# Top-32 attention and two feed-forward layers on one core: rounding moved to GpSimd, early scores finished sooner, first block's last steps put first

## The chip, the cores and the metric

The kernel runs on one core of a Trainium2 chip. The metric is the device time of one execution in microseconds, lower is better. Engines are called as in the profile: PE (TensorE matmul), PEld (its weight loads), DVE (VectorE), ACT (ScalarE), POOL (GpSimd) and SP (SyncE, which issues the DMAs).

## The reference

```python
def _attn_ref(q, k, v):                       # (4, 8, 576, 64) each
    scores = scale * np.matmul(q, k.transpose(0, 1, 3, 2))
    kth = np.partition(scores, -top_k, axis=-1)[..., -top_k:-top_k + 1]      # top_k = 32
    scores = np.where(scores >= kth, scores, -1000000000.0)
    attn = np.exp(scores - np.max(scores, axis=-1, keepdims=True))
    attn = attn / (np.sum(attn, axis=-1, keepdims=True) + 1e-09)
    return np.matmul(attn, v)
x = attn_out as (2304, 512)
x = np.maximum(x @ w_in, 0.0) ** 2 @ w_out            # layer 0: (512, 2048), (2048, 512)
h = x @ w_in2; return np.maximum(0.01 * h, h) @ w_out2    # layer 1
```

The weights come as 64-bit floats; the kernel rebuilds 32-bit ones on the chip.

## The kernel before

**Precision.** Every float32 operand of the large matmuls is used as two rounded parts, a high one (`split_hi`: the value written in the rounded format) and a low one (value minus high part, on POOL). `split_hi` runs on ACT where its flag is set, else on POOL. The flag is set for the head pairs with index in `HI_SET`, here the indices 0 to 15.

**Attention.** Four batches, four head pairs each. Rows are cut into units (`UNITS`); a unit and a head pair make a `uh`, a `uh` has tiles of 128 score rows by 576 columns, two tiles are a pair. There are 72 pairs, and each has 16 slots. In 14 of them DVE searches the 32 largest of a row, 8 at a time: per tile four `DVE.max` (L829) and three `DVE.match_replace` (L831). The loop over slots is the program's backbone; everything else is put on a slot with `at(slot, fn)`. What follows a pair's search: `shifts` (POOL, L288 and L289, the tile nb), `drop` (ACT, L295) and `expo_sum` (ACT, L299), `recip` (sum on POOL, L303; 1/sum on DVE, L304), `pt_main` and `pt_left` (PE transposes, ACT copies to PT), `av` (PE, values), `x_out` (DVE product xn, L428; ACT xh, L429; POOL xl, L432).

**Scores.** Batches 0 and 1 are direct: their scores are made 30 slots (`DLEAD`) before their search. Batches 2 and 3 (`EARLY`) are made ahead, spread over the slots of `FILL`, evicted to the tile stage and stored to DRAM (sd), to be loaded later. The rounded keys are KT (direct) and KTa (early). In PSUM the early scores have `SPB` banks (sp), the direct ones of batch 0 have `SDB` (sd), and three banks (att) serve the rest.

**Layers.** The 2304 rows are taken in blocks of 512, 256, 384, 512, 256, 384. Once a block's x is complete (`ready`), `moe(j, layer)` adds 16 steps for each layer: 12 matmuls into h (L575), activation on ACT, the low part gl on POOL, and 3 matmuls for each of `na` accumulators (L618 or L620). Block 0 consists of units 0 and 1, thus of the pairs 0 to 15; its slot `rslot[0]` is that of the last `x_out`. In the first 32 steps the weights are new: each has two raw tiles (wraw, 512 KB) that go through two ACT passes (L509, L510), two DVE passes (L514, L515), an ACT rounding (L519) and a POOL subtraction (L521), and are stored to DRAM (wd) for later blocks. The weights of the steps 0 and 1 are converted before the block is ready (`convert_now`).

**Order.** On each engine the instructions run in the order of the program. That order is made when the kernel is built, by a scheduler that takes priorities: what an event emits has an offset of `SOON` (100).

Of the kernel before, what the change touches and what calls it, by code (L numbers as in the profile page):

```python
# [8 lines left out]
F = mybir.dt.float32  # L9
R = mybir.dt.float32r  # L10
U = mybir.dt.uint32
AF = mybir.ActivationFunctionType
OP = mybir.AluOpType
# [6 lines left out]
H_SCALE = 2.0 ** -112  # L20


L_SCALE = 2.0 ** -29 * (1 - 2.0 ** -21)
L_BIAS = -0.499999
# [7 lines left out]
BLOCKS = [512, 256, 384, 512, 256, 384]  # L32
# [8 lines left out]
NATIVE = 3  # L41

EARLY = (2, 3)
FILL = (2, 245)
KPB = 2
NST = 3
SDB = 2
SPB = 3

NS = 6  # L50
NE = 4
# [1 line left out]
WCB = 4  # L53
# [3 lines left out]
DLEAD = 30  # L57
LEAD = 24

SOON = 100  # L60
CONVP = 30

HI_SET = (0, 1, 2, 3, 4, 5, 6, 7, 8, 9, 10, 11, 12, 13, 14, 15)
KLO_D = ((0, 0), (0, 1))
QLO_D = (0,)

# [5 lines left out]
def topk_attention_moe_moe2_kernel(  # L72
# [10 lines left out]
    B, NHP, _, _, S = q.shape  # L83
    D = v.shape[-1]
    P = 128
    DM, NF = 2 * NHP * D, w1.shape[0]
    NK = DM // P
    HALF = S // 2
# [5 lines left out]
    PE, ACT, DVE, POOL, SP = nc.tensor, nc.scalar, nc.vector, nc.gpsimd, nc.sync  # L94

    const = ctx.enter_context(tc.tile_pool(name="const", bufs=1))
    pool = ctx.enter_context(tc.tile_pool(name="work", bufs=2))
# [9 lines left out]
    def behind(key):  # L107

        return tc.issue_after(cur[key].ins) if key in cur else ExitStack()

    def split_hi(dst, src, act=False):
        if act:
            ACT.activation(dst, src, AF.Copy)
            return
        POOL.tensor_scalar(dst, src, 1.0, 1.0, op0=OP.mult, op1=OP.mult)
# [7 lines left out]
    uhs = []  # L123
    tiles = []
    for u in units:
        for hp in range(NHP):
            n = u["n"]
            uh = dict(u=u, hp=hp, n=n, b=u["b"], first=(u["t0"] == 0), ti=len(tiles), idx=len(uhs),
                      c0=P * (hp % 2) if n == 64 else 0)
            offs = (W - 64 - n, 64)  # L130
            for t in range(2 * n // P):
                lo, hi = t * P, t * P + P
# [11 lines left out]
    def direct(uh):  # L144
        return uh["b"] not in EARLY
# [4 lines left out]
    def split(uh):  # L150
        return uh["u"]["i"] >= NATIVE
# [4 lines left out]
    stage_psum = ahead_ctx.enter_context(tc.tile_pool(name="stage_psum", bufs=1, space=bass.MemoryType.PSUM))  # L156
    qsets = []
    for i in range(4):
        x = const if i < 2 else ahead
# [28 lines left out]
    def at(slot, fn, *a):  # L188
        events.setdefault(slot, []).append((fn, a))


    KT = {}

# [64 lines left out]
    def scores(t, half):  # L258
        uh = t["uh"]
        d = uh["qs"]  # L260
        kt = KT[uh["b"], uh["hp"]]
        if half == 0:
            if direct(uh):
                t["s"] = sbufs[t["i"] % NS]
            else:
                t["s"] = ahead.tile([P, S], F, tag="stage", name="stage", bufs=NST)
        ks = slice(half * HALF, (half + 1) * HALF)
        mm = [(x[:, h, c:c + P], kt[:, h, ks]) for h, c in t["parts"] for x in d]
        if not direct(uh):
            ps = stage_psum.tile([P, 512], F, tag="sp", name="sp", bufs=SPB)  # L270
        elif uh["b"] == 0:
            ps = stage_psum.tile([P, 512], F, tag="sd", name="sd", bufs=SDB)
        else:
            ps = bank()
        for i, (l, r) in enumerate(mm):
            PE.matmul(ps[:, 0:HALF], lhsT=l, rhs=r, start=i == 0, stop=i == len(mm) - 1)  # L276
        ACT.activation(t["s"][:, ks], ps[:, 0:HALF], AF.Copy)  # L277
        if half == 1 and not direct(uh):
            t["sd"] = dram.tile([P, S], F, tag=f"sd{t['i']}", name=f"sd{t['i']}")
            SP.dma_start(t["sd"], t["s"])  # L280
# [188 lines left out]
    wraw = {}  # L469

    def w_alloc(i):
        wi = pool.tile([P, 2, 512], R, tag="wi", name="wi", bufs=3)
        wo = pool.tile([P, 2, 512], R, tag="wo", name="wo", bufs=4)
        wt[i] = (wi, wo)
        return wi, wo
# [16 lines left out]
    def w_convert(i):  # L492
        g = w_convert_steps(i)
        while True:
            with tc.high_priority(offset=CONVP):
                if next(g, 1):
# [3 lines left out]
    def w_convert_steps(i):  # L500
# [3 lines left out]
        for raw, w in zip(wraw.pop(i), w2):  # L504
# [16 lines left out]
            POOL.tensor_tensor(w[:, 1, :], c, w.bitcast(F)[:, 0, :], op=OP.subtract)  # L521
            yield 0

    def w_store(i):
        if i >= len(steps) or not fresh[i]:
            return
        wi, wo = wt[i]
        d = wdram[steps[i][1:]]
        SP.dma_start(d[:, 0:2, :], wi.bitcast(F))
        SP.dma_start(d[:, 2:4, :], wo.bitcast(F))  # L530
# [123 lines left out]
    for uh in uhs:  # L654
        b, hp, i = uh["b"], uh["hp"], uh.get("di")
        z = score_slot(uh["ti"])
# [49 lines left out]
    for n, key in enumerate(keys):  # L706
        ks = [(0, load_k, (*key, held[key]))]
# [9 lines left out]
        if n + 1 < len(keys):  # L717
            nk = keys[n + 1]
            ks = [(0, load_k, (*nk, held[nk]))]
# [7 lines left out]
    for _ in range(2):  # L727
        at(FILL[0] - 1, request)
    done = 0
    for w, fn, args in fill:  # L730
        at(FILL[0] + (FILL[1] - FILL[0]) * done // total, fn, *args)
        done += w

    pairs = []
    for p in range(NPAIRS):
        pr = dict(t=tiles[2 * p:2 * p + 2], p=p)
        pairs.append(pr)
        z = 16 * p
        for i, t in enumerate(pr["t"]):
            if direct(t["uh"]):  # L740
                at(z - DLEAD + 5 * i, scores, t, 0)
                at(z - DLEAD + 2 + 5 * i, scores, t, 1)
            else:
                at(z - LEAD + i, load_s, t)
            if i == 0:
                at(z + 14, shifts, pr)
            at(z + 14 + i, drop, pr, i)
            at(z + 16 + i, expo_sum, pr, i)
            if split(t["uh"]):
                at(z + 20 + i, norm, pr, i)  # L750
            at(max(z + 20 + 3 * i, z + 21 + i), pt_main, t)
        at(z + 18, recip, pr)
        at(z + 26, pt_left, pr)
    rslot = [None] * len(blocks)
# [8 lines left out]
    for uh in uhs:  # L763
        if split(uh):
            za, z = 16 * (uh["lastA"] // 2) + 30, 16 * (uh["last"] // 2) + 30
            at(za, av_split, uh, 0)
            at(z + 2, av_split, uh, 1)
            z += 4
            at(z, x_out, uh, (0, 1))
            rmark(uh, z)  # L770
            continue
        apart = uh["n"] > P and uh["n"] % P and uh["ti"] % 2 == 0
        for hs in ((0,), (1,)) if apart else ((0, 1),):
            z = 16 * (uh["lastA"] // 2 if hs == (0,) else uh["last"] // 2) + 30
            nq = 2 * len(hs)
            for i in range(nq):
                at(z + i, av, uh, hs, i)
            at(z + nq, x_out, uh, hs)
        z += nq
        if uh["u"]["i"] == NATIVE - 1 and uh["hp"] == NHP - 1:  # L780
            at(z, open_late)
        rmark(uh, z)
# [6 lines left out]
        for _ in w_convert(i):  # L789
            pass  # L790

    at(rslot[0] - 80, w_raw, 0)
    at(rslot[0] - 80, w_raw, 1)
    at(rslot[0] - 28, convert_now, 0)
    at(rslot[0] - 27, w_raw, 2)
    at(rslot[0] - 14, convert_now, 1)
    at(rslot[0] - 13, w_raw, 3)
    at(rslot[0] - 10, w_store, 0)

    active = []  # L800
    credit = 0.0
# [11 lines left out]
    last = max(events)  # L813
    while slot <= last:
        p, i = divmod(slot, 16)
        if slot >= 0 and p < NPAIRS:
            pr = pairs[p]
# [6 lines left out]
            x = i % 2  # L824
            t = pr["t"][x]
# [9 lines left out]
        for fn, a in events.pop(slot, []):  # L835
            nr = len(ready)
            with tc.high_priority(offset=SOON):
                fn(*a)
# [66 lines left out]
```

## Time and profile before

| | before |
|---|---|
| median of 3 runs | 1211.68 us (1209.5 to 1212.38) |
| profiled execution, its own time | 1210.15 us |
| its span, first to last instruction | 1208.4 us |
| PE busy | 94% |
| DVE, ACT, POOL busy | 78%, 67%, 57% |
| mean granted TensorE clock | 0.98 |

Busy shares are averages over stages that differ: the attention of the first block alone, then attention and layers together, then layers alone. A matmul's recorded duration is longer than the time that it takes of PE, since matmuls overlap; the distance between starts tells that time. The profiled execution is 1.5 us below the median of the runs.

### The profile page before, as it was taken

How to read it: one execution, taken by the hardware profiler on the slowest of the kernel's cores; microseconds unless marked ns; L12 is line 12 of the kernel's file. 1: busy time of each engine (PE TensorE's matmuls, PEld its weight loads, DVE VectorE, ACT ScalarE, POOL GpSimd, SP SyncE). 2: the span in 40 equal slices, each digit the busy share in tenths (PEclk: the TensorE clock that was granted, in tenths of full speed). 3: DMA queues.
4: the chain of work that ended last, by engine and by line, in shares of the span. 5: the costliest groups of instructions: out<-in, count | busy, mean ns of one | idle time of the engine just before them, and what ended most of it. 6: DMA issues, size and time to landing. Idle time of an engine off the chain costs nothing.

```text
span 1208.4 us, 20261 instructions
## 1 busy us (share of the span) xinstructions
PE 1135.8 (94%) x6388; PEld 992.5 (82%) x6388; DVE 946.5 (78%) x1944; ACT 807.5 (67%) x1831; POOL 682.8 (57%) x982
## 2 busy tenths in 40 slices
PE   4988987999889999999999999999999999999998
PEld 3776765887678779988999898888788899999997
DVE  7999899868988999999999999999999930110122
ACT  6988898878998986766656666555666653334322
POOL 7765564877878876556666665555565644004300
PEclk9899897999999999999999999999999999999999
DMA  9765566779989888879988888776676679779974
GB/s 307 255 217 192 192 220 222 267 233 333 342 280 319 305 267 263 296 269 384 355 293 290 298 272 286 221 227 226 201 239 211 199 255 369 253 253 341 356 256 135
DMA packets 110522, 323.25 MB, mean 268 GB/s; under 512 B 17488, under 2 KB 25680, under 8 KB 110416
## 3 DMA queue, kind: packets, MB, share of 16 engines
q1 hardware_dynamic: 107776, 317.24, 77.5%
q10 hardware_dynamic: 2640, 4.72, 1.1%
q8 instruction: 52, 0.85, 0.3%
q14 instruction: 54, 0.44, 0.1%
HBM read 254.54 MB, written 67.37 MB: 266 GB/s over the span
## 4 chain that ended last, share of the span: by engine, by line
PE 71%; ACT 11%; DVE 7%; DMA 6%; issue 2%; POOL 1%; ACTq 0%; SPq 0%; POOLq 0%; DVEq 0%
PE h L575 29%; PE acc L620 14%; PE acc L618 14%; PE att L408 4%; PE att L313 4%; DVE m L829 3%; PE att L397 3%; DVE w L831 3%; DMA wraw<-in_w_dram 2%; DMA sd<-stage 2%; ACT stage L277 1%; ACT e L299 1%; ACT e L295 1%; ACT s L277 1%; PE sp L276 1%
## 5 line engine op out<-in xcount | busy, mean ns | idle before, releaser
L575 PE MATMUL h<-xh,wi 128*128 128x512 f32 (+2 forms) x1280 | 349.9, 345 | 13.4 <-ACT gb L597 4.2
L829 DVE MAX8 m<-w 128x8 f32<-128x576 f32 x432 | 311.9, 748 | 1.1
L575 PEld LDWEIGHTS h<-xh,wi 128*128 128x128 f32 x1280 | 227.5, 191 | 42.6 <-ACT gb L597 5.8
L831 DVE MATCH_REPLACE8 w<-m,w 128x576 f32<-128x576 f32 x288 | 213.5, 744 | 0.8
L575 PE MATMUL h<-xl,wi 128*128 128x512 f32 (+2 forms) x640 | 207.6, 342 | 0.6 <-DVE xl L632 0.6
L601 POOL TENSOR_TENSOR gl<-ga,gh 128x512 fp32r<-128x512 f32 (+2 forms) x160 | 162.7, 1017 | 37.9 <-ACT gh L600 32.1
L618 PE MATMUL acc<-gh,wo 128*128 128x512 f32 (+2 forms) x768 | 156.8, 340 | 0.0
L620 PE MATMUL acc<-wo,gh 128*128 128x512 f32 x576 | 152.5, 399 | 2.9 <-ACT gh L600 2.7
L598 POOL TENSOR_TENSOR ga<-ga,gb 128x512 f32<-128x512 f32 (+2 forms) x80 | 81.4, 1017 | 130.6 <-ACT gb L597 127.3
L618 PEld LDWEIGHTS acc<-gh,wo 128*128 128x128 f32 x768 | 126.5, 189 | 11.0 <-ACT gh L586 0.2
L575 PEld LDWEIGHTS h<-xl,wi 128*128 128x128 f32 x640 | 121.4, 191 | 12.3 <-DVE xl L632 1.1
L295 ACT ACTIVATE e<-s,m 128x576 f32<-128x576 f32 x144 | 111.7, 779 | 18.6 <-DVE m L829 13.4
L620 PEld LDWEIGHTS acc<-wo,gh 128*128 128x128 f32 x576 | 104.3, 189 | 24.1 <-ACT gh L600 5.0
L829 DVE MAX8 m<-s 128x8 f32<-128x576 f32 x144 | 104.1, 748 | 12.5 <-ACT s L277 6.1
L299 ACT ACTIVATE e<-e,nb 128x576 f32<-128x576 f32 x144 | 111.0, 774 | 3.2 <-POOL nb L289 2.8
L587 POOL TENSOR_TENSOR ga<-ga 128x512 f32<-128x512 f32 (+2 forms) x80 | 66.1, 827 | 78.1 <-ACT gh L586 72.8
L831 DVE MATCH_REPLACE8 w<-m,s 128x576 f32<-128x576 f32 x144 | 107.1, 744 | 0.6
L313 PE MATMUL att<-ident,e 128*128 128x128 f32 x576 | 90.8, 281 | 13.7 <-ACT e L299 5.1
L313 PEld LDWEIGHTS att<-ident,e 128*128 128x128 f32 x576 | 70.0, 143 | 27.4 <-ACT e L299 10.1
L308 POOL TENSOR_SCALAR e<-e,rc 128x576 f32<-128x576 f32 x108 | 79.8, 749 | 22.5 <-DVE rc L304 21.1
L585 ACT ACTIVATE ga<-h 128x512 f32<-128x512 f32 (+2 forms) x80 | 39.0, 488 | 77.4 <-PE h L575 71.9
L618 PE MATMUL acc<-gl,wo 128*128 128x512 f32 (+2 forms) x384 | 87.7, 345 | 0.1
(94 smaller groups left out, 2136.7 us busy)
## 6 DMA issues: line engine op xcount, KB each, us to landing
wi<-wd SPq DMA_DIRECT2D x160, 512.0 KB, 5.0
wo<-wd SPq DMA_DIRECT2D x160, 512.0 KB, 5.2
wraw<-in_w_dram SPq DMA_DIRECT2D x64, 512.0 KB, 6.0
sd<-stage SPq DMA_DIRECT2D x72, 288.0 KB, 2.9
s<-sd SPq DMA_DIRECT2D x72, 288.0 KB, 4.6
wd<-wi SPq DMA_DIRECT2D x32, 512.0 KB, 5.4
wd<-wo SPq DMA_DIRECT2D x32, 512.0 KB, 5.9
kraw<-in_k_dram SPq DMA_DIRECT2D x16, 576.0 KB, 5.4
```

The costliest lines, as they stand in the source:

```text
L295: ACT.activation(t["e"], t["s"], AF.Prelu, bias=pr["m8"][:, i, 31:32], scale=-1.0, alpha=0.125 / FAR)
L299: ACT.activation(e, e, AF.Exp, bias=pr["nb"][:, i:i + 1], scale=-FAR, accum_out=pr["sum"][:, i:i + 1])
L308: POOL.tensor_scalar(e, e, pr["rc"][:, i:i + 1], 1.0, op0=OP.mult, op1=OP.mult)
L313: PE.transpose(ps[:, j * P:(j + 1) * P], t["e"][:, j * P:(j + 1) * P], ident)
L575: PE.matmul(h[:, 0:n], lhsT=wi[:, w, c * P:(c + 1) * P], rhs=x[c][y][:, 0:n], start=cnt == 0, stop=cnt == 3 * NK - 1)
L587: POOL.tensor_tensor(a[:, 0:n], a[:, 0:n], a[:, 0:n], op=OP.mult)
L598: POOL.tensor_tensor(a[:, 0:n], a[:, 0:n], b[:, 0:n], op=OP.subtract)
L601: (DVE if j >= GLD else POOL).tensor_tensor(gl[:, 0:n], a[:, 0:n], gh.bitcast(F)[:, 0:n], op=OP.subtract)
L618: PE.matmul(acc[c][:, 0:n], lhsT=wo[:, w, cs], rhs=g[:, 0:n], start=first, stop=last)
L620: PE.matmul(acc[c], lhsT=g[:, cs], rhs=wo[:, w, :], start=first, stop=last)
L829: cur["dve"] = DVE.max(out=m8[:, x, 8 * r:8 * r + 8], in_=t["s"] if r == 0 else t["w"])
L831: cur["dve"] = DVE.match_replace(out=t["w"], in_to_replace=m8[:, x, 8 * r:8 * r + 8], in_values=t["s"] if r == 0 else t["w"], imm_value=NEG)
```

## The change

- `HI_SET` shrinks to the indices 0 and 1. The high parts of queries, direct keys and values with higher indices are made on POOL.
- The early scores are done by slot 215 instead of 245. A tile's two halves lie in one PSUM tile of two banks, and one ACT instruction evicts both. `SPB` is 2 such tiles (4 banks, before 3), `SDB` is 1 bank (before 2).
- Pair 15 (`first_done`) has its `shifts`, `drop`, `expo_sum`, `recip`, `pt_main` and `pt_left` emitted at its slots 13 and 14, with priority 800. Its `uh` is taken in two halves (`apart`), the second with priority. `rslot[0]` becomes slot 257 (before 274).
- The conversion of the weights of steps 0 and 1 is cut in two: the ACT passes at the slots 218 and 232, with the result in an sp tile, and the rest (`lead_bits`: DVE passes, rounding on POOL, subtraction) at slot 253.

```diff
-FILL = (2, 245)
+FILL = (2, 215)
-SDB = 2
-SPB = 3
+SDB = 1
+SPB = 2
+URGENT = 800
-HI_SET = (0, 1, 2, 3, 4, 5, 6, 7, 8, 9, 10, 11, 12, 13, 14, 15)
+HI_SET = (0, 1)
+    def urgent(fn):
+        def run(*a):
+            with tc.high_priority(offset=URGENT):
+                fn(*a)
+        return run
...
-            ps = stage_psum.tile([P, 512], F, tag="sp", name="sp", bufs=SPB)
+            if half == 0:
+                t["ps"] = stage_psum.tile([P, 2, 512], F, tag="sp", name="sp", bufs=SPB)
+            ps = t["ps"][:, half]
...
-        ACT.activation(t["s"][:, ks], ps[:, 0:HALF], AF.Copy)
+        if direct(uh):
+            ACT.activation(t["s"][:, ks], ps[:, 0:HALF], AF.Copy)
+        elif half == 1:
+            ACT.activation(t["s"].rearrange("p (x c) -> p x c", x=2), t.pop("ps")[:, :, 0:HALF], AF.Copy)
...
+    def lead_bits(i):
+        for b, vu, w in led.pop(i):
+            with behind("dve"):
+                DVE.scalar_tensor_tensor(b, vu, 3, b, op0=OP.logical_shift_left, op1=OP.bitwise_or)
+            DVE.scalar_tensor_tensor(b, vu, 0x80000000, b, op0=OP.bitwise_and, op1=OP.bitwise_or)
+            split_hi(w[:, 0, :], b.bitcast(F))
+            POOL.tensor_tensor(w[:, 1, :], b.bitcast(F), w.bitcast(F)[:, 0, :], op=OP.subtract)
...
+        if p == first_done:
...
+            at(z + 13, urgent(shifts), pr)
+            for i in range(2):
+                at(z + 13, urgent(drop), pr, i)
+                at(z + 13, urgent(expo_sum), pr, i)
+            at(z + 13, urgent(recip), pr)
+            for i in range(2):
+                at(z + 14, urgent(pt_main), pr["t"][i])
+            at(z + 14, urgent(pt_left), pr)
+            continue
...
-        apart = uh["n"] > P and uh["n"] % P and uh["ti"] % 2 == 0
+        tight = uh["last"] // 2 == first_done
+        apart = uh["n"] > P and (uh["n"] % P or tight) and uh["ti"] % 2 == 0
...
+            z = 16 * (uh["lastA"] // 2 if hs == (0,) else uh["last"] // 2) + (15 if near else 27 if tight and apart else 30)
...
-    at(rslot[0] - 80, w_raw, 0)
-    at(rslot[0] - 80, w_raw, 1)
-    at(rslot[0] - 28, convert_now, 0)
-    at(rslot[0] - 27, w_raw, 2)
-    at(rslot[0] - 14, convert_now, 1)
-    at(rslot[0] - 13, w_raw, 3)
-    at(rslot[0] - 10, w_store, 0)
+    for i, z in enumerate((218, 232)):
+        at(z - 40, w_raw, i)
+        at(z, lead_passes, i)
+        at(16 * first_done + 13, lead_bits, i)
+        at(rslot[0] - 30 + i, w_raw, i + 2)
+    at(rslot[0] - 1, w_store, 0)
```

**Place 1: DVE, end of the search of pair 15.** Before, pair 15 is m8_2438 and pair 16 is m8_2536; wc are weight tiles of steps 0 and 1.

```order
L831 MATCH_REPLACE w_2441<-m8_2438,w_2441 128x576
L829 MAX m8_2438<-w_2442 128x8
L829 MAX m8_2438<-w_2441 128x8
L304 RECIPROCAL rc_2314<-sum_2313 128x2
L514 SCALAR_TENSOR_TENSOR wc_2462<-att_2463,wc_2462 128x512
L831 MATCH_REPLACE w_2442<-m8_2438,w_2442 128x576
L514 SCALAR_TENSOR_TENSOR wc_2470<-att_2471,wc_2470 128x512
L831 MATCH_REPLACE w_2539<-m8_2536,s4_105 128x576
L515 SCALAR_TENSOR_TENSOR wc_2462<-att_2463,wc_2462 128x512
L829 MAX m8_2438<-w_2442 128x8
```

After the change, on DVE at the same place, pair 15 is m8_2205 and pair 16 is m8_2351.

```order
L881 MATCH_REPLACE w_2209<-m8_2205,w_2209 128x576
L879 MAX m8_2351<-s3_104 128x8
L881 MATCH_REPLACE w_2354<-m8_2351,s2_103 128x576
L879 MAX m8_2205<-w_2209 128x8
L879 MAX m8_2351<-w_2354 128x8
L881 MATCH_REPLACE w_2209<-m8_2205,w_2209 128x576
L881 MATCH_REPLACE w_2354<-m8_2351,w_2354 128x576
L879 MAX m8_2205<-w_2209 128x8
L553 SCALAR_TENSOR_TENSOR wc_2076<-sp_2077,wc_2076 128x512
L553 SCALAR_TENSOR_TENSOR wc_2158<-sp_2159,wc_2158 128x512
```

The weight passes that stood ahead of the pair's last MAX8 stand behind it now.

**Place 2: DVE, from pair 15's reciprocal to the last xn of block 0.** Before, they are rc_2440 and xn_2566.

```order
L304 RECIPROCAL rc_2440<-sum_2439 128x2
L831 MATCH_REPLACE w_2540<-m8_2536,w_2540 128x576
L831 MATCH_REPLACE w_2539<-m8_2536,w_2539 128x576
L829 MAX m8_2536<-w_2540 128x8
L829 MAX m8_2536<-w_2539 128x8
L831 MATCH_REPLACE w_2540<-m8_2536,w_2540 128x576
L428 TENSOR_TENSOR xn_2566<-att_2528,rb_2420 128x256
```

After the change, on DVE, they are rc_2207 and xn_2370, which holds one head of the pair.

```order
L316 RECIPROCAL rc_2207<-sum_2206 128x2
L881 MATCH_REPLACE w_2586<-m8_2583,s4_105 128x576
L879 MAX m8_2351<-w_2355 128x8
L879 MAX m8_2583<-w_2586 128x8
L881 MATCH_REPLACE w_2355<-m8_2351,w_2355 128x576
L526 SCALAR_TENSOR_TENSOR wc_2382<-att_2383,wc_2382 128x512
L881 MATCH_REPLACE w_2586<-m8_2583,w_2586 128x576
L879 MAX m8_2351<-w_2355 128x8
L440 TENSOR_TENSOR xn_2370<-att_2347,rb_2280 64x256
```

Seven instructions stand between the two, before it was five.

**Place 3: POOL, from pair 15's sum to the last xl of block 0.** Before, they are sum_2439 and the xl of xn_2566, one behind the other.

```order
L289 TENSOR_SCALAR nb_2524<-nb_2524 128x2
L255 TENSOR_TENSOR q10_78<-qraw_2427,q00_77 128x256
L521 TENSOR_TENSOR wo_2461<-wc_2470,wo_2461 128x512
L303 TENSOR_SCALAR sum_2439<-sum_2439 128x2
L432 TENSOR_TENSOR xl0_653<-xn_2566,xh0_652 128x256
```

After the change, on POOL, they are sum_2206 and the xl of xn_2370 (L116 is `split_hi`, wi and wo are the weights of steps 0 and 1).

```order
L315 TENSOR_SCALAR sum_2206<-sum_2206 128x2
L116 TENSOR_SCALAR wo_2075<-wc_2080 128x512
L556 TENSOR_TENSOR wi_2074<-wc_2076,wi_2074 128x512
L116 TENSOR_SCALAR wo_2157<-wc_2162 128x512
L556 TENSOR_TENSOR wi_2156<-wc_2158,wi_2156 128x512
L556 TENSOR_TENSOR wo_2075<-wc_2080,wo_2075 128x512
L116 TENSOR_SCALAR KT_3061<-kraw_3062 128x576 x2
L556 TENSOR_TENSOR wo_2157<-wc_2162,wo_2157 128x512
L245 TENSOR_TENSOR KT_3061<-kraw_3062,KT_3061 64x576
L300 TENSOR_TENSOR nb_2554<-m8_2351 128x2
L245 TENSOR_TENSOR KT_3061<-kraw_3062,KT_3061 64x576
L444 TENSOR_TENSOR xl0_647<-xn_2370,xh0_646 64x256
```

The conversion's last part and a direct key's rounding stand between the sum and the last xl.

## Rows read from the trace of the kernel before

**Rows 1.** The page's part 1: busy us, share of the span, instructions

```profile
PE 1135.8 (94%) x6388; PEld 992.5 (82%) x6388; DVE 946.5 (78%) x1944; ACT 807.5 (67%) x1831; POOL 682.8 (57%) x982
```

**Rows 2.** Busy time by stretch: window, its length, PE, PEld, DVE, ACT, POOL, PE clock, DMA

```profile
190.00:200.00 10.00, 9.08 (x27) 6.33 (x28) 10.00 (x22) 7.14 (x16) 3.70 (x6) 0.58 0.64 209
250.00:400.00 150.00, 138.91 (x663) 112.08 (x662) 124.68 (x233) 132.73 (x274) 121.94 (x129) 0.98 0.87 304
```

**Rows 3.** The chain that ended last: start us, us, what

```profile
150.66 0.53 PE sd L276 x4
...
215.69 2.80 PE acc L618 x12
```

**Rows 4.** Timeline of PE: start us, us, operation, idle before and its releaser

```profile
203.68 1.43 PE L575 MATMUL h<-xh,wi 128*128 128x512 f32 x5 [0.87 <-ACT xh L429]
204.94 1.07 PE L575 MATMUL h<-xl,wi 128*128 128x512 f32 x4
```

**Rows 5.** Timeline of DVE, end of pair 15's search to block 0's last xn

```profile
177.75 0.68 DVE L515 SCALAR_TENSOR_TENSOR wc<-att,wc 128x512 uint32<-128x512 uint32 x1
178.35 0.68 DVE L514 SCALAR_TENSOR_TENSOR wc<-att,wc 128x512 uint32<-128x512 uint32 x1
...
187.47 1.41 DVE L829 MAX8 m<-w 128x8 f32<-128x576 f32 x2
188.80 0.15 DVE L304 RECIPROCAL rc<-sum 128x2 f32<-128x2 f32 x1
...
192.10 0.75 DVE L829 MAX8 m<-w 128x8 f32<-128x576 f32 x1
...
201.68 0.42 DVE L428 TENSOR_TENSOR xn<-att,rb 128x256 f32<-128x256 f32 x1
```

**Rows 6.** Timeline of POOL: nb, sum and xl behind pair 15

```profile
192.94 0.20 POOL L288 TENSOR_TENSOR nb<-m 128x2 f32<-128x2 f32 x1 [4.62 <-DVE m L829]
...
197.53 0.19 POOL L303 TENSOR_SCALAR sum<-sum 128x2 f32<-128x2 f32 x1 [1.08 <-ACT e L299]
203.71 0.74 POOL L432 TENSOR_TENSOR xl<-xn,xh 128x256 fp32r<-128x256 f32 x1 [6.00 <-ACT xh L429]
```

**Rows 7.** POOL by line and shape: busy us, mean ns, idle before and releasers

```profile
L521 POOL TENSOR_TENSOR wi<-wc,wi 128x512 fp32r<-128x512 f32 x32 | 41.4, 1293 | 8.9 <-ACT wi L519 8.7
L255 POOL TENSOR_TENSOR q<-qraw,q 128x256 fp32r<-128x256 f32 x38 | 27.5, 732 | 5.4 <-ACT q L113 3.7 <-PE att L326 0.7
L238 POOL TENSOR_TENSOR KT<-kraw,KT 64x576 fp32r<-64x576 f32 x14 | 19.6, 1420 | 2.7 <-ACT KT L113 2.3
L115 POOL TENSOR_SCALAR KTa<-kraw 128x576 fp32r<-128x576 f32 x16 | 10.4, 670 | 1.9 <-DMA kraw<-in_k_dram 1.9
L115 POOL TENSOR_SCALAR q<-qraw 128x256 fp32r<-128x256 f32 x16 | 6.4, 404 | 11.0 <-PE sp L276 6.8 <-DMA qraw<-in_q_dram 4.0
```

**Rows 8.** ACT by line and shape, same columns

```profile
L277 ACT ACTIVATE s<-sd 128x288 f32<-128x288 f32 x72 | 27.8, 424 | 2.8 <-PE sd L276 2.6
...
L113 ACT ACTIVATE KT<-kraw 128x576 fp32r<-128x576 f32 x16 | 10.2, 699 | 2.8 <-DMA kraw<-in_k_dram 2.8
L113 ACT ACTIVATE q<-qraw 128x256 fp32r<-128x256 f32 x24 | 9.8, 431 | 3.0 <-DMA qraw<-in_q_dram 2.4 <-PE att L276 0.4
```

**Rows 9.** Timeline of ACT: two evictions of early scores, and what follows

```profile
178.38 0.77 ACT L277 ACTIVATE stage<-sp 128x288 f32<-128x288 f32 x2
178.96 0.85 ACT L295 ACTIVATE e<-s,m 128x576 f32<-128x576 f32 x1
```

**Rows 10.** Waits of POOL and of DVE, 0 to 204 us: total us, times, longest

```profile
POOL q L115 <- PE sp L276: 29.4, 14, 4.1
...
DVE m L829 <- ACT e L295: 5.6, 4, 2.8
```

**Rows 11.** Timeline of ACT: first readings of h in step 0 and in step 32

```profile
206.70 0.57 ACT L585 ACTIVATE ga<-h 128x512 f32<-128x512 f32 x1
...
449.97 0.38 ACT L585 ACTIVATE ga<-h 128x256 f32<-128x256 f32 x1
```

More of the change, by code (lines that the diff above doesn't have):

```diff
@@ L522, in w_convert_steps, with lead_passes @@
             yield 0
+    led = {}
+    def lead_passes(i):
+        led[i] = []
+        for raw, w in zip(wraw.pop(i), w_alloc(i)):
+            lo, hi = raw[:, :, 0], raw[:, :, 1]
+            b = pool.tile([P, 512], U, tag="wc", name="wc", bufs=WCB)
+            if not led[i]:
+                vs = stage_psum.tile([P, 2, 512], F, tag="sp", name="sp", bufs=SPB)
+            v = vs[:, len(led[i])]
+            ACT.activation(b, lo, AF.Copy, scale=L_SCALE, bias=L_BIAS)
+            ACT.activation(v, hi.bitcast(F), AF.Copy, scale=H_SCALE)
+            led[i].append((b, v.bitcast(U), w))
+    def lead_bits(i):
[5 more added lines that the diff above has]
+            POOL.tensor_tensor(w[:, 1, :], b.bitcast(F), w.bitcast(F)[:, 0, :], op=OP.subtract)
     def w_store(i):
@@ L734, in topk_attention_moe_moe2_kernel @@
     pairs = []
+    first_done = next(uh["last"] // 2 for uh in uhs if uh["hp"] == NHP - 1 and uh["u"]["g0"] + uh["n"] >= BLOCKS[0])
     for p in range(NPAIRS):
@@ L738, in topk_attention_moe_moe2_kernel @@
         z = 16 * p
+        if p == first_done:
+            assert all(direct(t["uh"]) and not split(t["uh"]) for t in pr["t"])
+            for i, t in enumerate(pr["t"]):
+                at(z - DLEAD + 5 * i, scores, t, 0)
+                at(z - DLEAD + 2 + 5 * i, scores, t, 1)
+            at(z + 13, urgent(shifts), pr)
[7 more added lines that the diff above has]
+            continue
         for i, t in enumerate(pr["t"]):
@@ L771, in topk_attention_moe_moe2_kernel @@
             continue
-        apart = uh["n"] > P and uh["n"] % P and uh["ti"] % 2 == 0
+        tight = uh["last"] // 2 == first_done
+        apart = uh["n"] > P and (uh["n"] % P or tight) and uh["ti"] % 2 == 0
         for hs in ((0,), (1,)) if apart else ((0, 1),):
-            z = 16 * (uh["lastA"] // 2 if hs == (0,) else uh["last"] // 2) + 30
+            near = tight and hs[-1] == 1
+            z = 16 * (uh["lastA"] // 2 if hs == (0,) else uh["last"] // 2) + (15 if near else 27 if tight and apart else 30)
             nq = 2 * len(hs)
             for i in range(nq):
-                at(z + i, av, uh, hs, i)
-            at(z + nq, x_out, uh, hs)
+                at(z + i, urgent(av) if near else av, uh, hs, i)
+            at(z + nq, urgent(x_out) if near else x_out, uh, hs)
         z += nq
```

## The prediction

> **What bounds the kernel now.** The page's shares come first: PE is busy for 94% of the span [rows 1]. That alone does not say that PE is the bound, because recorded matmuls overlap. The chain that ended last gives PE's true price: 12 matmuls of 512 columns take 2.80 us, 0.233 each, and 4 of 288 columns 0.53 us, 0.133 each [rows 3]. Pricing every matmul of the program by its columns like this gives 806 us for the layers and 238 us for attention, 1044 us in a span of 1208.
>
> So some 160 us are lost, and the question is where. Before the first block is ready, PE has little to do. Layer work starts in earnest when the last piece of the block's x arrives: PE waits for xh and issues the first long run of h at 203.68, the part with xl at 204.94 [rows 4]. PE's wait shows in its clock as well, 0.58 from 190 to 200 us [rows 2]. From there PE has 806 us of layers and 146 us of attention left, 952 us for 1004 us. A good part of the difference lies in the first 32 steps, where new weights are converted: h of step 0 is read at 206.70, h of step 32 at 449.97 [rows 11]; that is 243.3 us for 211.8 us of PE work. ACT is busy for 133 of 150 us there, POOL for 122 [rows 2]. After step 32 the steps take what PE needs, within a few us.
>
> The reader should see two things. The end is a PE sum that starts when block 0's x is complete, so an earlier start is passed on to the end unless the 32 converting steps eat it. And what comes before that start is paced by DVE, which is busy for all of 190 to 200 us [rows 2] and walks through its searches in program order.
>
> **When pair 15's search ends.** Two MAX8 start 1.33 us before the next instruction, 0.665 us each [rows 5]; a MATCH_REPLACE with its value load has the same distance. A weight pass takes 0.60 us, from one start to the next [rows 5]. The last MAX8 of pair 15 ends at 192.85 (192.10 and 0.75, rows 5), and nb follows at once [rows 6]. Counting DVE's order up to that MAX8: 138 MAX8, 103 MATCH_REPLACE and 7 weight passes before, 131, 98 and none after. The difference is 12 x 0.665 + 7 x 0.60 = 12.2 us, so the search would end at 180.65, if DVE waits as much as it does now.
>
> **What stands behind it.** Before, xn starts 8.8 us after that end, at 201.68 [rows 5], and xl ends 11.6 us after it, at 204.45 [rows 6]. After the change two queues have to be walked through.
>
> DVE has 14 searches, 9 weight passes, the other half of xn and a reciprocal ahead of the last xn: 14 x 0.665 + 9 x 0.60 + 0.5 = 15.2 us. The passes that were ahead of the search now stand here, so 6.4 of the 12.2 us are given back at once.
>
> POOL has more. From pair 15's nb to the end of the last xl I count: 4 instructions of 0.2 us (nb, sum) [rows 6]; a query's high part, 0.40; 4 high parts of keys, 0.67 each; 2 low parts of queries, 0.73; 4 low parts of keys, 1.42; 4 subtractions of weights, 1.29 [all rows 7]; 4 weight roundings of 512 columns, which the trace does not show on POOL. Those lie between 0.40 (256 columns) and 0.67 (576) and I take 0.62, near the wider. Two xl, 0.74 each [rows 6], close the list. The sum is 0.8 + 0.4 + 2.7 + 1.5 + 5.7 + 5.2 + 2.5 + 1.5 = 20.2 us, rounded. So the last xl would end at 180.65 + 20.2, about 200.8: 3.7 us earlier than now. The sum of pair 15, on which its reciprocal waits, is itself 8.6 us into that queue, where it came 4.7 us after the search before (197.53, rows 6).
>
> **PE's remaining work.** In PE's order the attention matmuls ahead of the first h add up to 92.3 us before and 94.6 us after, by the prices of rows 3. So 2.3 us less are left when the layers start. By step 32 the two orders are level (129.3 and 129.0). Start and remainder give 3.7 + 2.3 = 6.0 us.
>
> **The other edits.** Rounding moved from ACT to POOL: 20 query halves of 256 columns, 8 of 64, 12 key halves and 8 value halves. On ACT they took 0.43 and 0.70 us [rows 8], on POOL 0.40 and 0.67 [rows 7]; with the narrow ones scaled that is an estimated 22 us that changes engine, most of it before the start. ACT gains room, and POOL has idle time to take it. I put no direct gain or loss on it, with two ends: the four waits of DVE's MAX8 for ACT's drop, 5.6 us [rows 10], could all go; and POOL could be late, which is a rival below. Early scores evicted by tile: two evictions of 288 columns pass in 0.58 us (178.38 to 178.96, rows 9). No row shows one of 576 columns from two banks. It can't be shorter than one half, 0.29, and the nearest row with 576 columns lasts 0.85 [rows 9], so the 72 tiles give ACT between 21 us back and 19 us more. The columns are the same, so I take nothing; the 22 us of rounding that ACT loses cover the bad end, and if that cover were gone the fill would be late, not the search. Finishing the fill 30 slots sooner only pulls PE work into its idle time. The weights of steps 2 and 3 are loaded 3 to 17 slots earlier relative to the start, no cost.
>
> One bank for the direct scores of batch 0 instead of two: a half's matmuls wait for the eviction of the half before, 0.42 us each, 72 times [rows 8], up to 30 us of PE in a stretch where it idles. The trace before shows ACT waiting for PE at sd for 2.6 us in all [rows 8], so two banks were not scarce, and the scores are made 30 slots, 20 us, ahead of the search. I take zero and keep the 30 us for a rival.
>
> **The sum.** The profiled execution took 1210.15 us, so 1204.2 by its own time; the median of the runs is 1.5 us higher, which gives 1205.7.
>
> **The rivals.** *A larger gain.* If POOL runs ahead of my count (nb of pair 16 and the key's rounding not waiting), DVE's queue decides: xl ends at 180.65 + 15.2 + 1.1 = 197.0, 7.5 us earlier; with 2.3 us of PE work and the 5.6 us of ACT waits gone that is 15.4 us, 1196.3. Against it: POOL's list above has no slack, its instructions are in order, and one key's rounding needs a DMA.
>
> *The gain is swallowed while weights are converted.* In steps 8 to 16 of the layers POOL's order holds 61.8 us of work by the durations of rows 7, before 53.1; PE's holds 59.6. POOL would be the bound there for 8.7 us more than before, and the time 1205.7 + 4 to 8.7, that is 1210 to 1214.4. For it: that stage loses 31.5 us already, and vraw, the values for the second stage, loads at an attention slot that does not come earlier. Against it: over all 32 steps POOL's work grows by 3 us only, ACT's not at all.
>
> *Slower: POOL feeds the search late.* Now it waits 14 times for PE before it may overwrite an early query, 29.4 us in all, up to 4.1 us each [rows 10]. The direct keys and queries stood on ACT and passed these waits; now 12 key halves and most queries queue behind them. If scores arrive after DVE wants them, each wait goes through in full. From three such waits on (12.3 us, more than the 6.0 won and 3.6 of measurement) the kernel is slower: 1218, with four 1222. Against it: the 20 us that scores are made ahead; several waits have to pile up.
>
> *Slower: one bank starves PE.* If all of the 30 us of sd waits came in a row, scores would be more than their 20 us late, and DVE would wait for the other 10: 1205.7 + 10 = 1216. It decides only from 20 us on, and the waits are spread over some 160 us of PE's time, so it gets 0.04. The Trainium skill ("Perfetto Trace Analysis", Optimization Strategy) says that a gap that keeps repeating on an engine can mean too few PSUM buffers for the next tile. By that rule one bank would show as regular PE gaps at sd; no row here shows one bank.
>
> *The change does not do what it says* would be a start at 203 us as now, with pair 15's priority spent on POOL's queue: 1210 to 1212. It ends where the swallowed gain ends, and I count it there.
>
> **How the numbers follow.** No change is within 0.3%, 3.6 us, of 1211.7: 1208.1 to 1215.3. The forecast (a gain of 3.6 to 9 us) gets 0.45, the larger gain 0.15, the swallowed gain 0.24, the slower cases 0.16 (0.12 and 0.04). That makes faster 0.60, same 0.24, slower 0.16. The likeliest case alone spans 1202.5 to 1208. The range reaches from the larger gain, 1197, to the upper end of the swallowed one, 1215; the slower cases are left out.
>
> **What would show it.** Right: pair 15's last MAX8 ends near 181 us, its sum on POOL 8 us later, the last xl near 200 to 201, and h of step 0 is read near 203; the distance between the readings of steps 0 and 32 stays near 243 us. The first step fails if DVE waits for scores before 180 us longer than now. The second fails if xl comes sooner than 17 or later than 23 us after the search. The third fails if the 32 steps take over 247 us, with POOL or ACT as the releaser of PE. I would be wrong on the whole if the start moved by 6 us and the end did not.

## The result and the profile after

The changed kernel takes 1224.48 us (median of 4 runs, 1223.71 to 1225.17), the kernel before 1210.59 beside it (4 runs). The ratio is 1.0113, 95% interval 1.0095 to 1.013: slower, and outside the range of the prediction. The profiled span is 1221.9 us. Part 1 of its page answers to [rows 1]:

```profile
PE 1142.2 (93%) x6388; PEld 994.0 (81%) x6388; DVE 950.7 (78%) x1945; ACT 789.0 (65%) x1708; POOL 707.9 (58%) x1035
```

ACT has 18.5 us less to do and POOL 25 more. The totals don't say where 14 us come from. The waits from 0 to 204 us do; in [rows 10] DVE's dearest wait for ACT was for `e`, 5.6 us.

```profile
POOL q L116 <- PE sp L285: 17.6, 9, 3.1
POOL q L116 <- PE sd L285: 16.7, 7, 6.4
...
DVE m L879 <- ACT s L287: 12.1, 11, 2.3
ACT s L287 <- PE sd L285: 11.5, 15, 0.9
PE sd L285 <- ACT s L287: 11.5, 23, 1.1
```

PE waits 23 times for ACT to empty the bank `sd`, ACT waits 15 times for PE to fill it, and DVE waits 11 times for the scores. Before, the first MAX8 of a tile waited for ACT's scores once, 1.3 us. POOL's waits before it may overwrite a query, the prediction's other slow case, are 34.3 us in all where they were 29.4 [rows 10]. What the ping-pong looks like is seen on PE's timeline, three groups of direct scores of 0.8 us each, the later two held back by the eviction:

```profile
189.69 0.77 PE L285 MATMUL sd<-KT,q 128*128 128x288 f32 x4
191.05 0.77 PE L285 MATMUL sd<-KT,q 128*128 128x288 f32 x4 [0.59 <-ACT s L287]
192.32 0.80 PE L285 MATMUL sd<-KT,q 128*128 128x288 f32 x4 [0.50 <-ACT s L287]
```

How late the scores come is seen in the next view. After the change, ACT's eviction of a second half and DVE's first MAX8 of that tile:

```profile
135.05 0.40 ACT L287 ACTIVATE s<-sd 128x288 f32<-128x288 f32 x1
```

```profile
135.48 0.76 DVE L879 MAX8 m<-s 128x8 f32<-128x576 f32 x1 [2.32 <-ACT s L287]
```

The search starts 0.03 us behind the eviction, after 2.32 us of waiting. In the kernel before, the two evictions of a tile (x2, the second done at 123.55) and its first MAX8 lie 14.9 us apart:

```profile
122.84 0.71 ACT L277 ACTIVATE s<-sd 128x288 f32<-128x288 f32 x2
```

```profile
138.48 0.76 DVE L829 MAX8 m<-s 128x8 f32<-128x576 f32 x1 [2.85 <-ACT e L295]
```

Pairing the n-th second eviction with the n-th first MAX8 over the 36 direct tiles of batch 0, the median time from the end of the one to the start of the other, the lead of the scores, is 8.6 us before and 0.5 after. PE's order and ACT's eviction show where the second half is held up. The first half of this tile's scores is made at 127.11; the second needs the same bank, has twenty AV matmuls and a group of early scores ahead of it in PE's order, and comes at 133.62:

```profile
127.11 0.43 PE L285 MATMUL sd<-KT,q 128*128 128x288 f32 x2
127.38 0.74 PE L285 MATMUL sp<-KTa,q 128*128 128x288 f32 x4
127.95 5.06 PE L409 MATMUL att<-PT,VN 128*128 128x256 f32 x20
132.95 0.80 PE L285 MATMUL sp<-KTa,q 128*128 128x288 f32 x4
...
133.62 0.51 PE L285 MATMUL sd<-KT,q 128*128 128x288 f32 x2
```

```profile
128.81 0.42 ACT L287 ACTIVATE s<-sd 128x288 f32<-128x288 f32 x1
```

The bank is empty again at 129.23, so 4.4 us of this delay are not a wait for it but the program's order, which was made for one bank.

DVE pays for it. Its busy time up to the end of pair 15's last MAX8, before (192.86 us) and after (192.27 us):

```profile
0.00:192.86 192.86, 150.32 (x818) 121.47 (x819) 177.27 (x379) 166.56 (x442) 125.04 (x219) 0.93 0.72 234
```

```profile
0.00:192.27 192.27, 152.68 (x806) 121.28 (x806) 168.82 (x354) 145.08 (x318) 126.07 (x236) 0.94 0.67 223
```

DVE has 25 instructions less ahead of that point and stands idle for 23.5 us instead of 15.6. Behind it, on DVE, POOL and ACT, for [rows 5, 6, 11]:

```profile
191.51 0.75 DVE L879 MAX8 m<-w 128x8 f32<-128x576 f32 x1
...
207.70 0.43 DVE L440 TENSOR_TENSOR xn<-att,rb 64x256 f32<-64x256 f32 x1
```

```profile
202.33 0.19 POOL L315 TENSOR_SCALAR sum<-sum 128x2 f32<-128x2 f32 x1
...
213.30 0.72 POOL L444 TENSOR_TENSOR xl<-xn,xh 64x256 fp32r<-64x256 f32 x1
```

```profile
214.91 0.60 ACT L619 ACTIVATE ga<-h 128x512 f32<-128x512 f32 x1 [0.54 <-PE h L609]
...
460.36 0.38 ACT L619 ACTIVATE ga<-h 128x256 f32<-128x256 f32 x1
```

Pair 15's search ends where it ended before, a longer queue stands behind it, and h of step 0 is read 8.2 us later. Step 32 is 10.4 us later, step 96 15.1, and the span's end 13.5. Of what is added behind step 0, 5.7 us come between the steps 64 and 88 (130.6 us for 124.8); what costs them there stays open.

### The profile page after: what moved, and what is told of

It reads as the page before. It is cut to its first block, busy times and chain, and to the rows that moved or that the text cites. A ratio compares the mean times of both kernels' runs of the same rounds, so it can differ in the third digit from the quotient of the medians.

```text
span 1221.9 us, 20170 instructions
## 1 busy us (share of the span) xinstructions
PE 1142.2 (93%) x6388; PEld 994.0 (81%) x6388; DVE 950.7 (78%) x1945; ACT 789.0 (65%) x1708; POOL 707.9 (58%) x1035
## 4 chain that ended last, share of the span: by engine, by line
PE 57%; ACT 2%; DVE 2%; DMA 1%; issue 0%; ACTq 0%; SPq 0%
PE h L609 25%; PE acc L652 13%; PE acc L654 12%; PE att L420 4%; PE att L325 3%; DMA wo<-wd 1%; DVE m L879 1%; PE att L338 1%; PE att L285 1%; DVE w L881 1%; ACT e L307 0%; ACT PTs L330 0%; ACT e L311 0%; ACT s L287 0%; ACT y L669 0%
## 5 line engine op out<-in xcount | busy, mean ns | idle before, releaser
L325 PE MATMUL att<-ident,e 128*128 128x128 f32 x576 | 90.2, 280 | 10.6 <-ACT e L311 8.4
```

The source lines that it names most:

```text
L325: PE.transpose(ps[:, j * P:(j + 1) * P], t["e"][:, j * P:(j + 1) * P], ident)
```

## The experiments

The medians, with the kernel before beside each on the same chip. The ratio is estimated from all the runs of both, so it can differ by a tenth of a per cent from that of the medians:

| kernel | edit | median us | before | ratio, 95% interval |
|---|---|---|---|---|
| b_sd1 | before, one bank for `sd` | 1221.13 | 1208.12 | 1.0103, 1.0085 to 1.0121 |
| b_banks | before, all bank edits | 1230.83 | 1209.46 | 1.0174, 1.0145 to 1.0203 |
| b_merge_half | b_banks, second half in a shared bank | 1209.16 | 1208.12 | 1.0004, 0.9991 to 1.0017 |
| b_round | before, rounding on POOL | 1212.93 | 1209.46 | 1.0033, 1.0017 to 1.0049 |
| b_fill | before, fill done by slot 215 | 1209.22 | 1209.46 | 1.0006, 0.9989 to 1.0023 |
| b_start | before, first block's early start | 1210.28 | 1209.46 | 1.0009, 0.9996 to 1.0021 |
| a_sd2 | changed, bank edits undone | 1211.9 | 1208.12 | 1.0033, 1.0009 to 1.0057 |
| a_half | changed, second half in a shared bank | 1218.95 | 1208.12 | 1.0089, 1.0062 to 1.0117 |
| a_half_act | a_half, rounding on ACT | 1213.3 | 1209.2 | 1.004, 1.0025 to 1.0054 |
| x_early | before, 16 extra MAX8 ahead of block 0 | 1215.72 | 1209.2 | 1.0065, 1.0039 to 1.0091 |
| x_less | before, 16 MATCH_REPLACE fewer behind it | 1204.47 | 1209.2 | 0.9955, 0.9936 to 0.9974 |
| x_late | before, 16 extra MAX8 behind step 96 | 1213.22 | 1209.2 | 1.0029, 1.0016 to 1.0041 |

### The bank of the direct scores

b_sd1 changes one number of the kernel before; b_banks makes that edit with the wide eviction in `scores` and SPB; b_merge_half takes the second half of b_banks's direct tiles out of the single bank.

```
b_sd1:         -SDB = 2
               +SDB = 1
b_merge_half:  -        elif uh["b"] == 0:
               +        elif uh["b"] == 0 and half == 0:
```

> The kernel before with one bank for the direct scores of batch 0 instead of two, nothing else; early scores keep three single banks and are evicted by halves. Theory single bank: PE and ACT wait for each other at the direct scores (PE 8 us or more), DVE waits for scores 8 us or more, and the time is 12 to 24 us over before, as with all the bank edits together. Theory wide eviction: the loss comes from the early scores' two-bank tiles, and this one stays within 4 us of before.

> The kernel before with the tile-wide eviction of early scores, two double banks for them and one bank for direct scores, nothing else. Theory banks: PE waits at the direct scores for ACT by 8 us or more (before under 1), DVE waits for scores by 8 us or more, and the time is 5 to 13 us over before. Theory GpSimd: within 4 us of before.

> The kernel before with the wide eviction of early scores and one bank for direct scores, as in the run of the bank edits, but a direct tile's second half goes to one of the three shared banks, so its matmuls need not wait for the eviction of the first half. Theory single bank: PE's waits at the direct scores fall under 4 us and the time comes back to within 5 us of before. Theory wide eviction: the time stays 12 us or more over before.

Waits from 0 to 204 us in b_sd1, in b_banks and in b_merge_half:

```profile
PE sd L276 <- ACT s L277: 12.7, 21, 1.0
...
ACT s L277 <- PE sd L276: 8.1, 9, 2.4
...
DVE m L829 <- ACT s L277: 5.1, 5, 2.1
```

```profile
PE sd L278 <- ACT s L280: 11.7, 22, 1.3
ACT s L280 <- PE sd L278: 11.3, 13, 2.1
DVE m L834 <- ACT s L280: 11.1, 11, 2.2
```

```profile
ACT s L280 <- PE sd L278: 2.7, 4, 1.0
...
PE sd L278 <- ACT s L280: 1.6, 3, 0.9
...
DVE m L834 <- ACT s L280: 1.5, 1, 1.5
```

One bank alone costs 1.03%, where the whole change costs 1.13%, with the change's ping-pong and late scores, though DVE waits for them 5.1 us and not the 8 expected. In b_merge_half a tile's halves again have two places; the three waits fall to near what they were before (2.6, 0.6 and 1.3 us), and the loss is gone, though `sd` still has one bank, SPB is 2 and the eviction is wide. So it is the two halves of one tile taking turns in one bank that costs, and not the wide eviction by itself: `stage<-sp` takes ACT 46.3 us after instead of 53.1. Together with the wide eviction one bank costs more, 1.74%, 21 us where 5 to 13 were expected; why more was not separated, and the shares of the edits don't add up.

The edit acts through the waits and through the program's order, which is built around the banks. DVE's busy time up to the last xn of block 0, before (201.68 us) and in b_sd1 (214.33 us), shows how much is which:

```profile
0.00:201.68 201.68, 159.06 (x846) 127.23 (x846) 186.09 (x398) 172.54 (x457) 128.74 (x225) 0.92 0.71 231
```

```profile
0.00:214.33 214.33, 166.78 (x848) 128.70 (x849) 196.49 (x412) 177.03 (x464) 129.42 (x228) 0.92 0.65 217
```

In b_sd1 this xn comes 12.6 us later. Only 2.2 us of that are more idle time of DVE. The other 10.4 are busy time, with 14 more instructions ahead of the xn, nine of them searches (MAX8 or MATCH_REPLACE, 6.3 us by the distance from start to start). So in b_sd1 a good part of the loss is the order that the scheduler makes for one bank. No run kept the order fixed while the bank was taken away, so what the waits cost by themselves is not shown.

### Rounding, fill, early start

```
b_round:  HI_SET = (0, 1)
b_fill:   FILL = (2, 215)
b_start:  of the diff: first_done, urgent, lead_passes, lead_bits, tight
          (SDB, SPB, scores, FILL, HI_SET as before; lead_passes keeps
          its intermediate in SBUF)
```

> The kernel before with the rounding moved to GpSimd alone. If GpSimd's queue makes direct scores late (theory GpSimd), DVE waits for scores rise from 1.3 us to 8 us or more before the first block is ready, and the time is 5 to 13 us over before. If the score banks are the cause (theory banks), DVE's waits stay within 3 us of before and the time within 4 us of it.

> The kernel before with the early scores done by slot 215 alone. If the tighter filling is the cause (theory fill), ACT waits for the storing DMA of early scores rise from 5 to 9 us or more, direct scores come late behind them, and the time is 5 us or more over before. By the theories banks and GpSimd: within 4 us of before.

> The kernel before with the early start alone: pair 15 with priority, its unit in halves, the first two weight conversions cut in two (their intermediate in SBUF). The rounding stays on ACT, the banks and the filling are as before. My step of the sum says that this part is worth 3 to 9 us: h of step 0 is read 3 to 9 us before 206.7 us, and the time is 3 to 9 us under before. If the work behind pair 15 on DVE and GpSimd takes all of it, both stay within 3 us of before.

The fill costs nothing, as predicted. The rounding costs 0.33%, where I took zero, inside the 4 us that theory banks allowed, and DVE waits for scores 1.9 us: GpSimd does not make them late. Its profiled execution (span 1208.6) is as long as that of before, so the place of the loss can't be read from it.

b_start is the prediction's first steps with the scores in time. The last xn, the last xl and the first reading of h, on DVE, POOL and ACT:

```profile
195.85 0.43 DVE L435 TENSOR_TENSOR xn<-att,rb 64x256 f32<-64x256 f32 x1
```

```profile
197.68 0.73 POOL L439 TENSOR_TENSOR xl<-xn,xh 64x256 fp32r<-64x256 f32 x1 [0.55 <-ACT xh L436]
```

```profile
203.52 0.57 ACT L615 ACTIVATE ga<-h 128x512 f32<-128x512 f32 x1
```

The last xl ends 6.0 us earlier (198.41 for 204.45, forecast 3.7) and h of step 0 is read 3.2 us earlier (203.52 for 206.70, rows 11). Step 8 is 8.2 us ahead. Step 16 is 2.4 us behind: between the two b_start takes 80.5 us, the kernel before 69.9. That whole stage before and in b_start, and the 20 us of it in which PE idles most:

```profile
263.85:333.79 69.94, 61.46 (x286) 48.25 (x284) 60.09 (x114) 62.55 (x128) 55.10 (x60) 0.98 0.90 323
```

```profile
255.66:336.16 80.50, 71.66 (x337) 58.12 (x335) 67.87 (x130) 70.34 (x148) 59.47 (x68) 0.92 0.85 295
310.00:330.00 20.00, 13.35 (x54) 10.10 (x52) 18.78 (x38) 18.60 (x41) 14.77 (x18) 0.83 0.93 332
```

In the 20 us PE is busy for 13.35 at a granted clock of 0.83; ACT and DVE are nearly full, and POOL, which the prediction named as the bound of this stage, is not. Over the whole stage every engine has more to do than before (ACT 7.8 us, DVE 7.8, POOL 4.4), and none is full: work that lay elsewhere before falls into it. So the early start is won, near its forecast size, and given back while weights are converted. Which engine bounds the stage was not tested.

### The changed kernel with edits undone

a_half has b_merge_half's line in the changed kernel; a_half_act has HI_SET of before as well; a_sd2 has SDB, SPB and `scores` of before, with the intermediate of lead_passes in SBUF.

> The changed kernel with the bank edits undone: early scores in three single banks, evicted by halves, two banks for direct scores; the first two conversions keep their intermediate in SBUF. If the bank edits are the whole loss, the last piece of block 0's x is ready 3 to 6 us before that of the kernel before (201.7 us for the last product on DVE), and the time is 0 to 6 us under before. If the rounding on GpSimd has a share of its own, the time is 2 to 6 us over before.

> The changed kernel with a direct tile's second half of scores in one of the three shared banks. Theory single bank: PE's 11.5 us of waits at the direct scores fall under 4 us, the last product of block 0 on DVE comes at 194 to 202 us (207.7 in the changed kernel), and the time is 8 to 16 us under that of the changed kernel. If the bank is only a symptom, both stay as they are within 4 us.

> The changed kernel with two edits undone: the second half of direct scores goes to a bank of its own kind again, and the rounding is back on ACT. Theory one (rounding on GpSimd is what is left of the loss of the kernel with only the first of the two undone, 1219): 1207 to 1212, and the first step of block 3 near 752. Rival (the loss comes from the order that the other edits make, not from the rounding): 1216 to 1220, first step of block 3 near 758.

With the banks as before, a_sd2 does what the prediction's first steps said: the last xn comes at 193.43, and h of step 0 is read at 198.9, 7.8 us earlier than before (forecast: 6.0). At step 96 it is level (753.5), and 0.33% is left. That is the size of what b_round costs alone; that it is the rounding is not shown by this, since a_half_act below is left with as much without it. The runs of a_sd2 scatter from 1206 to 1219 us.

With the second half moved (a_half), PE's waits at `sd` fall to 4.6 us, DVE waits for scores only 1.5 us, and the last xn comes at 197.0, in the range expected. But the time falls by 5.5 us, not by 8 to 16, and 0.89% is left. Undoing all the bank edits (a_sd2) takes away 0.80 of the 1.13 points, moving the half alone 0.24; a part of what makes the difference is open. About half of that (0.49 points) goes when the rounding returns to ACT. The two kernels differ from the start (h of step 0 at 204.9 in a_half, 198.4 in a_half_act) by 6.6 us, and by 7.0 at step 96. A place where a_half loses time ahead of block 0 is seen on its POOL and ACT:

```profile
169.70 1.31 POOL L116 TENSOR_SCALAR KT<-kraw 128x576 fp32r<-128x576 f32 x2 [2.67 <-DMA kraw<-in_k_dram]
171.09 1.40 POOL L245 TENSOR_TENSOR KT<-kraw,KT 64x576 fp32r<-64x576 f32 x1
172.57 0.20 POOL L300 TENSOR_TENSOR nb<-m 128x2 f32<-128x2 f32 x1
172.84 1.41 POOL L245 TENSOR_TENSOR KT<-kraw,KT 64x576 fp32r<-64x576 f32 x1
174.35 0.19 POOL L301 TENSOR_SCALAR nb<-nb 128x2 f32<-128x2 f32 x1
```

```profile
174.57 0.78 ACT L311 ACTIVATE e<-e,nb 128x576 f32<-128x576 f32 x1 [6.38 <-POOL nb L301]
```

The rounding of a direct key waits 2.67 us for its DMA, the two `nb` of a pair queue behind it, and ACT stands for 6.38 us. In a_half ACT waits for `nb` 10.7 us up to 204 us, in a_half_act 3.4. That is the prediction's rival of a late POOL, a wait behind an in-order rounding, though it reaches ACT and not the search first. It is not where a_half falls behind the kernel before: at step 88 a_half is still ahead (703.2 for 705.9), at step 96 behind (758.7 for 753.5).

a_half_act fell between what the two theories expected. It reads h of step 0 at 198.4, 8.3 us earlier than before, is 11.1 us ahead at step 88 (694.86 for 705.94) and ends no earlier. PE at the first step of block 3, step 96:

```profile
743.41 0.66 PE L325 MATMUL att<-ident,e 128*128 128x128 f32 x4 [4.68 <-POOL e L320]
...
752.36 0.80 PE L609 MATMUL h<-xh,wi 128*128 128x512 f32 x1 [3.98 <-ACT ga L619]
```

PE waits first for the normalised `e` of the attention ahead in its order, then for ACT to read h. The h that it waits for is made by 748.4; ACT reads it behind an `e` that waits for DVE's search:

```profile
748.79 0.77 ACT L307 ACTIVATE e<-s,m 128x576 f32<-128x576 f32 x1 [4.08 <-DVE m L879]
...
751.73 0.58 ACT L619 ACTIVATE ga<-h 128x512 f32<-128x512 f32 x1
```

So the layers, ahead of the search, are held to its pace by ACT's order. The granted clock falls with it. Windows of a_half_act and then of before:

```profile
744.00:752.00 8.00, 4.38 (x16) 3.18 (x14) 7.97 (x16) 3.81 (x9) 1.35 (x5) 0.71 0.49 181
752.00:757.00 5.00, 4.64 (x11) 3.68 (x12) 4.93 (x12) 1.71 (x3) 3.69 (x4) 0.50 0.43 147
```

```profile
744.00:752.00 8.00, 6.68 (x37) 5.26 (x36) 7.83 (x18) 5.80 (x13) 3.32 (x5) 1.00 0.78 246
752.00:757.00 5.00, 4.32 (x19) 3.18 (x18) 4.93 (x11) 1.99 (x5) 2.09 (x2) 1.00 0.97 369
```

The lead of 11.1 us at step 88 is 1.8 at step 96. b_merge_half (7.0 ahead at step 88, 1.6 at step 96) and a_half (2.8 ahead, then 5.2 behind) lose there too. An earlier first block is waited away where the search has not kept as far ahead. What keeps a_half_act 0.4% above before was not found: its step 128 is read at 973.6, 1.0 us later than before.

### What DVE's time is worth

```
x_early, x_late (p in 4..11, p in 60..67):
+                if r == 0 and p in range(4, 12):
+                    DVE.max(out=m8[:, x, 0:8], in_=t["s"])
                 cur["dve"] = DVE.max(out=m8[:, x, 8 * r:8 * r + 8], ...)
x_less:
-            elif i < 14:
+            elif i < 14 and not (r == 2 and p in range(20, 28)):
```

> The kernel before with a MAX8 of scores issued twice in the 16 tiles of pairs 4 to 11, ahead of block 0; nothing else is changed and the second result is the same. A MAX8 stands 0.665 us from the next instruction, so DVE has 10.6 us more to do before 180 us. Theory (DVE's search sets the end: in all ten kernels so far the end comes 238 to 246 us after the last MAX8): the last MAX8 comes about 10 us later, 979, and the median is 1218 to 1221. Rival one (PE's sum from block 0 on sets the end): the same, since block 0 is late as well. Rival two (lateness of DVE before block 0 is made up in the 32 converting steps): 1209 to 1212.

> The kernel before without the last MATCH_REPLACE in the 16 tiles of pairs 20 to 27, behind block 0 (left out: in these tiles the fourth group of eight maxima repeats the third, so fewer scores are dropped there than the reference drops). DVE has 16 x 0.665 = 10.6 us less to do between 230 and 530 us; block 0 starts as now. Theory (DVE's search sets the end): the last MAX8 comes up to 10 us earlier, 959 to 963, and the median is 1199 to 1204. Rival one (PE's sum from block 0 on sets the end, as the prediction had it): no change, 1207 to 1211.

> The kernel before with a MAX8 issued twice in the 16 tiles of pairs 60 to 67, between 820 and 930 us, behind the first step of block 3. Theory (the end follows the last MAX8): the last MAX8 near 979, the median 1218 to 1221. Rival one (PE's sum from block 0 on): 1208 to 1212. Rival two (only block 3's readiness, at 750 us, sets the time of the rest): 1208 to 1212 too, with the first step of block 3 where it is now, 753.

x_early and x_late add 10.6 us of DVE by [rows 5]. x_less takes away 11.5: a MATCH_REPLACE with its value load stands 0.72 us from the next instruction (before, 194.03 to 194.75 us on DVE), not 0.665 as the prediction and the expectation took it. The medians move by +6.5, -4.7 and +4.0 us: none is free, none goes through in full. x_less refutes that PE's sum from block 0 on sets the end, since block 0 starts as before (206.6) and 4.7 us less are needed. x_late refutes that block 3's readiness fixes the rest: its step 96 is read at 752.5, no later than before, and it ends later. The last MAX8 of before and of x_late:

```profile
969.19 0.76 DVE L829 MAX8 m<-w 128x8 f32<-128x576 f32 x1
```

```profile
980.72 0.76 DVE L831 MAX8 m<-w 128x8 f32<-128x576 f32 x1
```

The search ends 11.5 us later and the span 2.9 (the median 4.0), so the end does not simply follow the last MAX8 either. From block 0 to the last MAX8 (207 to 969 us of the kernel before) PE is busy for 97% and DVE for 94% of the time, and at block 3 PE waits for the search (a_half_act above). From step 136 on the search is over; from there to the end it takes 208 to 210 us in all these kernels.

## Why the prediction was wrong

**The step that failed: one bank, taken at zero.** The prediction read that ACT waited 2.6 us for PE at `sd` [rows 8], called two banks not scarce, and put the scores 20 us ahead of the search from the distance in slots. That wait is ACT's and says nothing of PE and DVE with half the room. By time the scores led by 8.6 us in the median, not 20, and 0.5 after. The rival "one bank starves PE" had the right place, and 0.04, because it was said to decide only from 20 us of PE's waits on. The row says 11.5 us of such waits, 23 of 0.5 us, and the kernel is 13.9 us slower: what counts is when the second half of a tile comes, not the sum of PE's waits. Nor is it all waiting: in b_sd1 a good part of the loss is the order that the scheduler makes for one bank. The rule of the Trainium skill ("Perfetto Trace Analysis", Optimization Strategy), that the same gap repeating on the engine that should be saturated can mean too little PSUM for the next tile, agrees with this trace: PE's 23 gaps at `sd` and DVE's 11 for the scores repeat, and in b_merge_half a second place for half a tile leaves 3 and 1. It was left aside for want of a row.

**The search's end, 180.65 forecast, 192.26 measured.** The text named its own condition, DVE waiting as much as now. DVE idles 23.5 us for 15.6, though its waits for `e` fall from 5.6 to 0.6 us as the better end of the rounding foresaw. That is 7.9 of the 11.6 us lost. The rest is busy time, which fell by 8.5 instead of 12.2. It is a cost of the waits too: a MAX8 that is followed by an idle gap counts its whole 0.75 us and not 0.667, and 28 of them are followed by one where 9 were. Counted from start to start without the gaps, a MAX8 takes 0.685 us on average for 0.670 and a MATCH_REPLACE 0.682 for 0.664, which makes 3.7 us.

**What stands behind the search was right.** From that end xn starts 15.4 us later (forecast 15.2), pair 15's sum comes after 10.1 (8.6), the last xl ends after 21.8 (20.2). Rounding 512 columns on POOL lasts 0.62 us (taken: 0.62). A queue counted in order from durations of the same engine held within 2 us.

**The end as a PE sum that starts at block 0 failed as well.** Even with its scores in time the early start brings nothing (b_start, 1.0009; a_sd2, 7.8 us earlier at step 0 and 1.0033). This is the prediction's own sign of being wrong on the whole, the start moving by 6 us and the end not. It kept the case as the swallowed gain (0.24), worked out as 8.7 us lost in steps 8 to 16 with POOL as the bound. b_start loses 10.6 there and the changed kernel 8.4, but POOL is busy for only 63.4 of the changed kernel's 78.3 us, so that the size agrees is luck. Beyond it the lead is waited away at block 3. The prediction followed the steps only to step 32 and said that behind it they take what PE needs, within a few us. By its own numbers 20.5 us were left there (52 us more than PE's work in all, 31.5 of them up to step 32), and x_less, which takes work from DVE alone, ends 4.7 us earlier. In the changed kernel steps 0 to 32 take 245.5 us, near the 243 forecast.

**The other edits.** The fill at zero was right. The wide eviction was bounded by 21 us back and 19 more; it gives ACT 6.8 us back, and no time. The rounding at zero was mis-sized: 0.33% alone, and 0.49 points between a_half and a_half_act.

## What to carry to other kernels

A buffer count is not judged by the waits that its present number shows, but by the lead that it gives: the time from a tile's last write to its first use, read on both engines' timelines. Here two halves of one tile that took turns in one PSUM bank left a median lead of 0.5 us, and DVE, which has little slack, paid for the late halves. Where a scheduler orders the program, a buffer count also changes that order, so compare the order as well as the waits.

Where two engines are both nearly full, an earlier start of one can be waited away at a later place where it needs the other; follow the gain past the stage where it is won. A known amount of one engine's work, added or taken away at a few places, gives the price of its time there.

## What the runs showed of the hardware

In a_half_act PE idled for 4.68 us up to 743.41 and for 3.98 us up to 752.36. The mean granted clock was 1.00 from 740 to 744 us, 0.71 from 744 to 752, with PE busy for 4.38 of these 8 us, and 0.50 (the lower of its two levels, 1.2 GHz) from 752 to 757. In the kernel before, PE was busy for 6.68 of the same 8 us and kept 1.00. So arriving early cost twice here: PE waited, and its next matmuls ran at the lower level, 0.43 us from start to start for 512 columns (752.95 to 755.94 us) where the higher level gives 0.233 [rows 3], until the clock was back, 0.94 by 757 to 762 us.
